# Attention and gated layers on one core: products of p and v of two pairs of units in one run, products of the first layer in pieces of one k-tile

## The chip, the cores and the metric

The kernel runs on one core of a Trainium2 chip. The metric is device time in microseconds (us), the median of several runs. Before the change it is 772.67 us (three runs: 772.47 to 773.61).

## The reference

A clustered attention over 2 x 8 heads (768 positions, 64 per head) is followed by two feed-forward blocks; all in float32.

```python
mask = q_assign[:, :, :, None] == k_assign[:, :, None, :]
scores = where(mask, (1/8) * q @ k.T, -1e9)
attn = exp(scores - max(scores)); attn = attn / (sum(attn) + 1e-9)
x = (attn @ v)                      # 16 heads -> [1536, 512]
a = x @ w1; b = x @ w2
x = (a * b @ w3) @ w_out            # d_ff 1024
h = x @ w_in                        # d_ff 2048
out = (maximum(h, 0) + alpha * minimum(h, 0)) @ w_out2
```

The assignments are the nearest of 16 centroids per head, by normalised products.

## The kernel before

**Units.** Attention is cut into 96 units: 16 heads by 6 query tiles of 128. One loop (line 762), written out by hand, gives every engine its order; an engine does its instructions in that order and waits on semaphores. In the turn of unit i TensorE (PE) transposes the weights p of unit i-4 (`emit_T`, L551, six transposes into two PSUM tiles `t` of three), then makes the scores of unit i+1 (`emit_S`, L511 and L512, four matmuls of 384 columns into a tile `s`), then possibly a step of other work ("fill"), and in even turns the products of p and v of one pair of units (`emit_PV`, L568: 12 matmuls of the program, 24 in the trace; two column tiles of 64, so the two units of a pair stand side by side in the array). The other engines: VectorE (DVE) takes the maximum of the scores (L519) and copies one half of the transposes (L559); ScalarE (ACT) does the exponential (L526) and copies the other half (L558); GpSimd (POOL) scales p by its sum (L537) and splits the next head's q and k. `emit_x` copies the products of a pair from PSUM to the rows `xr` (L580 on ACT, L581 on DVE).

**Fill.** Until unit 55 the fill steps are the cluster assignments. From unit 56 on they are the first layer of batch 0 (`l1`, L618): for every f of 8 blocks and every half a of 384 tokens one product with w1 (`l1a`) and one with w2 (`l1b`), each 4 k-tiles of three matmuls (L298 to L300, float32 split in a high and a low part), 12 matmuls in a step. The product l1a is copied from PSUM by ACT (`asb`, L627), the product l1b is multiplied with that copy by DVE (`pr`, L631). Before unit 96 both write the same tile: `alloc_f` (L679) gives the one PSUM bank `f`. All eight banks are given out: four to `s`, two to `t`, one to `o`, one to `f`. The condition in L783 puts one step in every odd unit until 16 are done (units 57 to 87); from unit 96 on there is a step in each unit, and those take turns with the two buffers of `s`.

**Weights.** `w_goal` moves the load and split of the weights on by one stage: ACT L185, L196 and L280, DVE L198, POOL L281.

After unit 103 the loop ends; the rest of the first layer and the later layers follow, TensorE work almost without a gap.

Of the kernel before, what the change touches and what calls it, by code (L numbers as in the profile page):

```python
# [8 lines left out]
F32 = mybir.dt.float32  # L9
# [7 lines left out]
B, H, S, D, NCL = 2, 8, 768, 64, 16  # L17
P = 128
NT = S // P
# [5 lines left out]
HS = S // 2  # L25
# [3 lines left out]
def kernel(  # L29
# [14 lines left out]
    nc = tc.nc  # L44

    cp = ctx.enter_context(tc.tile_pool(name="cp", bufs=1))
# [99 lines left out]
    def w_done(key):  # L146

        need[key] -= 1
# [136 lines left out]
    def w_goal(n):  # L285

        w_pairs(n)
        w_step(n)

    def w_ready(key):  # L290
        n = at[key]
        while in_ring[st["ring"]] <= n if seq[n][0] == "k" else st["conv"] <= ordinal[n]:
            w_pairs(n, True)
            if in_ring[st["ring"]] <= n or seq[n][0] == "c":
                w_step(n, True)

    def mm3(o, whi, wlo, xhi, xlo, first, last):
        nc.tensor.matmul(o, lhsT=whi, rhs=xhi, start=first, stop=False)  # L298
        nc.tensor.matmul(o, lhsT=whi, rhs=xlo, start=False, stop=False)  # L299
        nc.tensor.matmul(o, lhsT=wlo, rhs=xhi, start=False, stop=last)  # L300
# [4 lines left out]
    def pst(tag, shape, name, bufs=1):  # L305
        return ps.tile(shape, F32, tag=tag, name=name, bufs=bufs)
# [134 lines left out]
    ST, VS, hraw = {}, {}, {}  # L441

    def st_tile(name):
        return cp.tile([P, 4, S], F32R, tag="st", bufs=2, name=name)
# [8 lines left out]
    def v_load(p):  # L453
        if p < B * 4:
            VS[p] = ap.tile([P, 2, NT, D], F32, tag="vs", bufs=2, name=f"vs{p}")
            nc.sync.dma_start(out=VS[p], in_=vv[p // 4, p % 4])
# [39 lines left out]
    NU = B * H * NT  # L496
    scp, pt, sums, pth, ob, XR = {}, {}, {}, {}, {}, {}

    def unit(i):
        return i // NT, i % NT  # L500
# [21 lines left out]
    def emit_exp(i):  # L522
        if i % 2 == 0:
            sums[i // 2] = ap.tile([P, 2], F32, tag="sums", bufs=3, name=f"su{i}")
        p = ap.tile([P, S], F32, tag="p", bufs=6, name=f"p{i}")
        nc.scalar.activation(  # L526
            out=p.rearrange("p (a k) -> p a k", a=2), in_=scp.pop(i)[:, :, 0:HS], func=AF.Exp,
            bias=nmax.pop(i), scale=1.0, accum_out=sums[i // 2][:, i % 2 : i % 2 + 1],
        )
        pt[i] = p  # L530

    def emit_r(g):
        nc.vector.tensor_scalar(out=sums[g], in0=sums[g], scalar1=1e-9, scalar2=None, op0=ALU.add)
        nc.vector.reciprocal(out=sums[g], in_=sums[g])  # L534
# [8 lines left out]
    def emit_T(i):  # L543
        g, j = divmod(i, 2)
        if j == 0:
            pth[g] = ap.tile([P, NT, 256], F32, tag="pth", bufs=3, name=f"pt{g}")
        for a in range(2):
            t = pst("t", [P, 3, P], f"t{i}{a}", bufs=2)
            for k in range(3):
                kt = 3 * a + k  # L550
                nc.tensor.transpose(t[:, k], pt[i][:, kt * P : kt * P + P], ident)  # L551
            tps[i, a] = t
        pt.pop(i)
# [4 lines left out]
        nc.scalar.copy(out=pth[g][:, 0:3, q], in_=tps.pop((i, 0)))  # L558
        nc.vector.tensor_copy(pth[g][:, 3:6, q], tps.pop((i, 1)))  # L559

    def emit_PV(g):

        u, qt = unit(2 * g)
        ob[g] = pst("o", [P, P], f"o{g}")
        v = VS[u // 2]
        for kt in range(NT):
            for j in range(2):
                nc.tensor.matmul(  # L568
                    ob[g][64 * j : 64 * j + 64], lhsT=v[:, u % 2, kt], rhs=pth[g][:, kt, j * P : j * P + P],
                    start=(kt == 0), stop=(kt == NT - 1), tile_position=(0, 64 * j),  # L570
                )

    def emit_x(g):
        u, qt = unit(2 * g)
        o = ob.pop(g)
        p = u // 2
        if u % 2 == 0 and qt == 0:
            XR[p] = cp.tile([P, S], F32, tag=f"xr{p % 4}", name=f"xr{p}")
        mine = slice(0, 64) if u % 2 == 0 else slice(64, 128)
        nc.scalar.copy(out=XR[p][mine, qt * P : qt * P + P], in_=o[0:64])  # L580
        nc.vector.tensor_copy(XR[p][mine, qt * P + P : qt * P + 256], o[64:128])  # L581
        pth.pop(g)


    def lc(f, alloc, between):
# [23 lines left out]
    def l1_mm(t, b, f, m, a):  # L609
        hi, lo = his["l1", b, f, m]  # L610
        s = slice(a * HS, a * HS + HS)
        for kt in range(4):
            c = slice(kt * P, kt * P + P)
            mm3(t, hi[:, c], lo[:, c], XS[b][:, 0, kt, s], XS[b][:, 1, kt, s], kt == 0, kt == 3)
        if a == 1:
            w_done(("l1", b, f, m))

    def l1(b, f, a, alloc):  # L618

        if b == 1:  # L620
            PR[1] = PR[0]
        if b not in PR:
            PR[b] = cp.tile([P, 8 * S], F32, tag="pr", name=f"pr{b}").rearrange("p (f s) -> p f s", f=8)
        t = alloc(f"l1a{b}{f}{a}")
        l1_mm(t[:, 0:HS], b, f, 0, a)
        q = wp.tile([P, HS], F32, tag="asb", name=f"asb{b}{f}{a}")
        nc.scalar.copy(out=q, in_=t[:, 0:HS])  # L627
        yield
        t = alloc(f"l1b{b}{f}{a}")
        l1_mm(t[:, 0:HS], b, f, 1, a)  # L630
        nc.vector.tensor_tensor(out=PR[b][:, f, a * HS : a * HS + HS], in0=t[:, 0:HS], in1=q, op=ALU.mult)  # L631
        yield


    with tc.manual_schedule():
# [22 lines left out]
        for j in range(2):  # L658
            nc.vector.tensor_scalar(
                out=cpd[:, j], in0=ct, scalar1=cn2, scalar2=evod[:, j : j + 1], op0=ALU.mult, op1=ALU.mult  # L660
            )
        t = pst("s", [P, 2, 512], "cnt", bufs=2)[:, 0]
# [16 lines left out]
        def alloc_f(name):  # L679
            return pst("s", [P, 2, 512], name, bufs=2)[:, 0] if late else pst("f", [P, 512], name)  # L680

        def l1_steps(b, f, ahead):
            for a in range(2):
                if a == 0:
                    w_ready(("l1", b, f, 1))
                for _ in l1(b, f, a, alloc_f):
                    w_goal(ahead)
                    yield f

# [63 lines left out]
        nc.scalar.activation(out=warm, in_=warm, func=AF.Exp)  # L753
        nc.gpsimd.tensor_scalar(out=alp, in0=alp, scalar1=-1.0, scalar2=1.0, op0=ALU.mult, op1=ALU.mult)

        xdone, fill_at = [], [0]
        fill = fill_steps()

        LT = 4
        L1_B, L1_D = 16, 24  # L760
        NUH = NU // 2
        for i in range(NU + 8):
            if 0 <= i - LT < NU:
                emit_T(i - LT)
            if i + 1 < NU:
                emit_S(i + 1)

            if i >= 7 and i % 2 == 1 and (i - 7) // 2 < NU // 2:
                emit_x((i - 7) // 2)
            if i >= 2 and i % 2 == 0 and i // 2 - 1 < NU // 2:  # L770
                emit_r(i // 2 - 1)
            if 0 <= i - 2 < NU:
                emit_norm(i - 2)
            if 0 <= i - LT < NU:
                emit_evac(i - LT)
            if i + 1 < NU:
                emit_max(i + 1)
            if i < NU:
                emit_exp(i)
                u, j = unit(i)  # L780
                for k in ((0,), (1, 2), (3, 4), (), (5,), ())[j]:
                    h_split(u + 1, k)
            if i >= NU or i % 2 == 1 or i < 24 or 40 < i < 56:  # L783
                if fill_at[0] < (L1_B if i < NU else L1_D):
                    if next(fill) is not None:
                        fill_at[0] += 1
            fine[0] = i < NU - 1
            if 10 <= i < 54 and i % 2 == 0:
                w_goal(at["l1", 0, 2, 0])
            if NUH + 8 <= i < NU - 1 and i % 2 == 0:  # L790
                w_goal(at["l1", 0, fill_at[0] // 4, 0] + 3)
            if NUH + 4 <= i < NUH + 8:
                x_split(0, i - NUH - 4, 0)
                x_split(0, i - NUH - 4, 1)
                xdone.append(i)
            if i == NU - 1:
                late.append(i)
                for k in range(2):
                    w = st_tile(f"wo{k}").rearrange("p a n -> p (a n)").rearrange("p (g t n) -> p g t n", g=3, t=2)
                    for g in range(3):  # L800
                        WO[3 * k + g] = w[:, g, 0], w[:, g, 1]
            if i >= NU - 1:
                w_goal(at["wo", 0, 3, 0])

            k = i - 6
            if k >= 0 and k % 2 == 0 and k // 2 < NU // 2:
                emit_PV(k // 2)
                if k % 12 == 10:
                    v_load(k // 12 + 2)
        pscope.close()  # L810


# [26 lines left out]
        alloc_f = alloc_c  # L839
# [30 lines left out]
        x = cp.tile([P, 8 * S], F32, tag="wox", name="x2_1").bitcast(F32R).rearrange("p (t e s) -> p t e s", t=2, e=4)  # L870
        XF = [cp.tile([P, S], F32, tag=f"xr{e}", name=f"xf{e}") for e in range(4)]
        for b, a in ((0, 0), (0, 1), (1, 0), (1, 1)):
            s = slice(a * HS, a * HS + HS)
            for e in range(4):
                t = alloc_c(f"l2_{b}{e}{a}")
# [6 lines left out]
                if b == 1:  # L882
# [6 lines left out]
                    out=X2[b][1][:, e, s], in0=t[:, 0:HS], in1=f32(X2[b][0][:, e, s]), op=ALU.subtract  # L889
# [11 lines left out]
        x = x.rearrange("p t e s -> p (t e s)")  # L901
# [297 lines left out]
```

## Time and profile before

| | us |
|---|---|
| median of the runs | 772.67 |
| the profiled execution | 773.44 |
| its span, first to last instruction | 771.6 |
| TensorE busy in the span | 746.4 (97%) |
| VectorE, ScalarE, GpSimd busy | 464.6, 458.0, 270.1 |
| mean granted clock of TensorE | 0.99 of 2.4 GHz |

TensorE is the engine in which the time lies. Busy shares are means over the whole span; for the change the stretch of units 56 to 103 counts, about 166.8 to 309 us of the span. Matmuls are pipelined and the ends in the trace are modelled, so a matmul's cost is read from the distance of two starts. A row's start is counted from the start of the span.

### The profile page before, as it was taken

What the parts mean: (1) busy time and instruction counts of PE and PEld (TensorE: products, weight loads), DVE (VectorE), ACT (ScalarE), POOL (GpSimd) and SP (SyncE); (2) the same over time, 40 slices, a digit from 0 to 9 for tenths busy, and PEclk for the clock granted to TensorE, in tenths of its full rate; (3) what the DMA queues carried; (4) which work ended last, traced back from release to release, by engine and by line L of the source; (5) the groups of instructions that cost most, each with busy time, mean ns of one, the idle gap of its engine ahead of it and who ended that gap; (6) DMA issues with size and microseconds to landing.
All of it is one profiled execution on the core that took longest, in us unless ns stands there. A gap on an engine that the chain in (4) does not pass through costs nothing.

```text
span 771.6 us, 13292 instructions
## 1 busy us (share of the span) xinstructions
PE 746.4 (97%) x5025; PEld 675.7 (88%) x5025; DVE 464.6 (60%) x807; ACT 458.0 (59%) x946; POOL 270.1 (35%) x244
## 2 busy tenths in 40 slices
PE   5899999989999999999999999999999999999998
PEld 2787788879999989999999999999989998989886
DVE  3776798995666674357233446525645547776764
ACT  5687887675556675467344657647565544555443
POOL 0366576684555643243222432312211111221110
PEclk9799999999999999999999999999999999999999
DMA  7657466253534635756444497756655226433402
GB/s 251 193 177 224 108 173 166 67 123 79 150 110 135 186 119 168 236 217 223 160 164 164 161 316 251 282 181 231 206 201 164 110 110 232 177 114 135 163 0 82
DMA packets 39440, 129.41 MB, mean 168 GB/s; under 512 B 5232, under 2 KB 5360, under 8 KB 39376
## 3 DMA queue, kind: packets, MB, share of 16 engines
q1 hardware_dynamic: 39376, 128.56, 51.5%
q8 instruction: 40, 0.66, 0.3%
q14 instruction: 24, 0.20, 0.1%
HBM read 86.17 MB, written 28.31 MB: 148 GB/s over the span
## 4 chain that ended last, share of the span: by engine, by line
PE 86%; DMA 5%; DVE 3%; POOL 2%; ACT 2%; issue 1%; SPq 1%; POOLq 0%; ACTq 0%; DVEq 0%
PE o L568 6%; PE t L551 6%; PE l L298 6%; PE l L299 6%; PE acc L300 6%; PE acc L299 6%; PE l L300 6%; PE acc L298 6%; PE s L511 3%; PE s L512 3%; PE l1a L299 3%; PE l1b L298 3%; PE l1a L298 3%; PE l1a L300 3%; PE l1b L300 3%; PE l1b L299 3%
## 5 line engine op out<-in xcount | busy, mean ns | idle before, releaser
L281 POOL TENSOR_TENSOR wh<-wt,wh 128x512 fp32r<-128x512 f32 x57 | 74.2, 1301 | 169.7 <-ACT wh L280 165.0
L537 POOL TENSOR_SCALAR p<-p,su 128x768 f32<-128x768 f32 x96 | 88.4, 929 | 91.8 <-DVE su L534 42.4
L198 DVE SCALAR_TENSOR_TENSOR wt<-wu,wt 128x512 uint32<-128x512 uint32 x72 | 72.9, 1013 | 40.9 <-ACT wt L196 40.7
L519 DVE TENSOR_REDUCE nm<-s 128x1 f32<-128x768 f32 x96 | 91.5, 953 | 8.6 <-PE s L512 3.1
L526 ACT ACTIVATE p<-s,nm 128x768 f32<-128x768 f32 x96 | 87.1, 907 | 6.8 <-DVE nm L519 5.4
L551 PE MATMUL t<-cst,p 128*128 128x128 f32 x576 | 84.1, 281 | 3.6 <-DVE pt L559 1.6
L551 PEld LDWEIGHTS t<-cst,p 128*128 128x128 f32 x576 | 65.9, 143 | 15.8 <-issue 7.9
L511 PE MATMUL s<-st 128*128 128x384 f32 x192 | 74.9, 390 | 2.0 <-ACT p L526 1.5
L568 PE MATMUL o<-pt,vs 128*64 128x128 f32 x1152 | 73.5, 277 | 0.0
L568 PEld LDWEIGHTS o<-pt,vs 128*64 128x64 f32 x1152 | 61.9, 137 | 12.3 <-issue 12.1
L512 PE MATMUL s<-st 80*128 80x384 f32 x192 | 66.7, 347 | 0.2 <-DMA st<-mk 0.2
L558 ACT COPY pt<-t 128x384 f32<-128x384 f32 x96 | 45.9, 478 | 30.4 <-PE t L551 29.4
L559 DVE COPY pt<-t 128x384 f32<-128x384 f32 x96 | 52.8, 550 | 16.1 <-PE t L551 15.1
L244 POOL TENSOR_TENSOR sp<-sx,sp 128x512 fp32r<-128x512 f32 x16 | 22.4, 1420 | 107.9 <-ACT sp L241 107.5
L968 DVE SCALAR_TENSOR_TENSOR gr<-gr,alp 128x384 f32<-128x384 f32 x32 | 20.9, 652 | 49.1 <-ACT gr L967 49.1
L196 ACT ACTIVATE wt<-wr 128x512 uint32<-128x512 uint32 x72 | 48.3, 671 | 0.0
L185 ACT ACTIVATE wu<-wr 128x512 f32<-128x512 f32 x72 | 47.9, 666 | 0.0
L298 PE MATMUL l1a<-xs,wh 128*128 128x384 f32 x128 | 43.3, 338 | 1.3 <-DVE pr L631 0.7
L280 ACT CAST wh<-wt 128x512 fp32r<-128x512 f32 x57 | 35.4, 621 | 13.1 <-DVE wt L198 7.1
L298 PE MATMUL l1b<-xs,wh 128*128 128x384 f32 x128 | 43.1, 337 | 0.0
L299 PE MATMUL l1a<-xs,wh 128*128 128x384 f32 x128 | 43.0, 336 | 0.1
L631 DVE TENSOR_TENSOR pr<-l1b,asb 128x384 f32<-128x384 f32 x32 | 17.8, 555 | 42.1 <-PE l1b L300 24.3
(244 smaller groups left out, 1984.9 us busy)
## 6 DMA issues: line engine op xcount, KB each, us to landing
wr<-in_w_dram SPq DMA_DIRECT2D x48, 512.0 KB, 5.3
kept<-wh SPq DMA_DIRECT2D x41, 512.0 KB, 5.8
wh<-kept SPq DMA_DIRECT2D x39, 512.0 KB, 4.0
wr<-in_w3t_dram SPq DMA_DIRECT2D x16, 512.0 KB, 4.1
ywc<-kept SPq DMA_DIRECT2D x15, 512.0 KB, 3.5
jm<-in_qka_dram SPq DMA_DIRECT2D x12, 512.0 KB, 5.6
hr<-in_qkh_dram SPq DMA_DIRECT2D x16, 384.0 KB, 3.6
st<-st SPq DMA_DIRECT2D x16, 384.0 KB, 3.7
```

What stands on the lines that cost most here:

```text
L198: nc.vector.scalar_tensor_tensor(out=t, in0=u, scalar=3, in1=t, op0=ALU.logical_shift_left, op1=ALU.bitwise_or)
L281: nc.gpsimd.tensor_tensor(out=lo, in0=tts.pop(n), in1=f32(hi), op=ALU.subtract)
L298: nc.tensor.matmul(o, lhsT=whi, rhs=xhi, start=first, stop=False)
L299: nc.tensor.matmul(o, lhsT=whi, rhs=xlo, start=False, stop=False)
L300: nc.tensor.matmul(o, lhsT=wlo, rhs=xhi, start=False, stop=last)
L511: nc.tensor.matmul(t[:, a, 0:HS], lhsT=s[:, 0, q], rhs=s[:, 1, ks], start=True, stop=False)
L512: nc.tensor.matmul(t[:, a, 0:HS], lhsT=s[0:80, 2, q], rhs=s[0:80, 3, ks], start=False, stop=True)
L519: nc.vector.tensor_reduce(out=m, in_=scp[i][:, :, 0:HS], op=ALU.max, axis=AX.XY, negate=True)
L526: nc.scalar.activation(out=p.rearrange("p (a k) -> p a k", a=2), in_=scp.pop(i)[:, :, 0:HS], func=AF.Exp, bias=nmax.pop(i), scale=1.0, acc ...
L537: nc.gpsimd.tensor_scalar(out=pt[i], in0=pt[i], scalar1=sums[i // 2][:, i % 2 : i % 2 + 1], scalar2=1.0, op0=ALU.mult, op1=ALU.mult)
L551: nc.tensor.transpose(t[:, k], pt[i][:, kt * P : kt * P + P], ident)
L568: nc.tensor.matmul(ob[g][64 * j : 64 * j + 64], lhsT=v[:, u % 2, kt], rhs=pth[g][:, kt, j * P : j * P + P], start=(kt == 0), stop=(kt == N ...
```

## The change

Three edits. (1) From pair 26 on two pairs make one run: their 24 matmuls stand one behind the other at the end of a turn divisible by 4 (60, 64, ..., 100), into one tile `o` of two columns of blocks, and `emit_x` copies both together where they belong to the same head (one copy an engine, else two). In the turn behind such a run the exponential stands ahead of these copies on ACT. (2) The first layer's products give the loop back the turn after every k-tile, so a piece is three matmuls. (3) From unit 56 on pieces are given out by a counter: none in the turns divisible by 4, in the other three 6.4 / 3 each by addition (two, at times three); 64 pieces from unit 57 to unit 95, then four in every turn as before.

```diff
+    Q0 = 26
+    runs = [[g] for g in range(Q0)] + [[g, g + 1] for g in range(Q0, NU // 2, 2)]
+    run_at = {2 * r[-1] + 6: r for r in runs}
-    def emit_PV(g):
-        ob[g] = pst("o", [P, P], f"o{g}")
+    def emit_PV(r):
+        o = ob[r[-1]] = pst("o", [P, 2, P], f"o{r[0]}")
+        for k, g in enumerate(r):
...
+                        o[64 * j : 64 * j + 64, k], lhsT=v[:, u % 2, kt], rhs=pth[g][:, kt, j * P : j * P + P],
...
+            if g % 6 == 5:
+                v_load(g // 6 + 2)
...
+        for x, k in parts:
+            nc.scalar.copy(out=x[:, :, 0], in_=o[0:64, k])
+        for x, k in parts:
+            nc.vector.tensor_copy(x[:, :, 1], o[64:128, k])
...
         for kt in range(4):
+            if kt:
+                yield
             c = slice(kt * P, kt * P + P)
             mm3(t, hi[:, c], lo[:, c], XS[b][:, 0, kt, s], XS[b][:, 1, kt, s], kt == 0, kt == 3)
...
-            if i >= 7 and i % 2 == 1 and (i - 7) // 2 < NU // 2:
-                emit_x((i - 7) // 2)
+            if i - 1 in run_at:
+                if len(run_at[i - 1]) > 1 and i < NU:
+                    emit_exp(i)
+                emit_x(run_at[i - 1])
...
-            if i >= NU or i % 2 == 1 or i < 24 or 40 < i < 56:
-                if fill_at[0] < (L1_B if i < NU else L1_D):
-                    if next(fill) is not None:
-                        fill_at[0] += 1
+            if len(xdone) < 4:
+                if i % 2 == 1 or i < 24 or 40 < i < 56:
+                    next(fill)
+            else:
+                npc[0] += 0 if i % 4 == 0 and i < NU else 4 if i >= NU else 6.4 / 3
+                while npc[0] > 0.999 and fill_at[0] < (L1_B if i < NU else L1_D):
+                    npc[0] -= 1
+                    if next(fill) != "piece":
+                        fill_at[0] += 1
...
-            k = i - 6
-            if k >= 0 and k % 2 == 0 and k // 2 < NU // 2:
-                emit_PV(k // 2)
-                if k % 12 == 10:
-                    v_load(k // 12 + 2)
+            if i in run_at:
+                emit_PV(run_at[i])
```

**Place 1.** TensorE around pairs 26 and 27 (turns 58 to 61), before: `o26` and `o27` are the products of p and v, `t` transposes, `s` scores; left out stand the rest of the scores and a step of `l1b000`.

```order
L512 MATMUL s59_2302<-st9_1967 128x384
L568 MATMUL o26_2319<-pt26_2216,vs4_1701 64x128 x12
L551 MATMUL t550_2332<-cst_69,p55_2208 128x128 x3
...
L512 MATMUL s61_2377<-st10_2166 128x384
L568 MATMUL o27_2396<-pt27_2293,vs4_1701 64x128 x12
L551 MATMUL t570_2409<-cst_69,p57_2276 128x128 x3
```

The same place in the changed kernel:

```order
L512 MATMUL s61_2355<-st10_2166 128x384
L573 MATMUL o26_2374<-pt26_2216,vs4_1701 64x128 x12
L573 MATMUL o26_2374<-pt27_2285,vs4_1701 64x128 x12
L551 MATMUL t570_2399<-cst_69,p57_2276 128x128 x3
L551 MATMUL t571_2403<-cst_69,p57_2276 128x128 x3
```

The products of pair 26 moved two turns down, to those of pair 27; the scores of unit 59 are now followed by a piece and then by transposes.

**Place 2.** TensorE where the product l1a of block 1 (first half of the tokens, `l1a010`) ends and l1b (`l1b010`) begins, before, with the semaphores waited for:

```order
L300 MATMUL l1a010_2592<-xs0_2096,wh2_1194 128x384
L551 MATMUL t620_2611<-cst_69,p62_2470 128x128 [waits Activation_49,Pool_49]
...
L512 MATMUL s67_2619<-st11_2392 128x384
L568 MATMUL o30_2641<-pt30_2524,vs5_2114 64x128 x12
...
L512 MATMUL s68_2662<-st11_2392 128x384
L298 MATMUL l1b010_2679<-xs0_2096,wh3_1407 128x384
```

The same place in the changed kernel (turn 69):

```order
L300 MATMUL l1a010_2611<-xs0_2096,wh2_1194 128x384
L298 MATMUL l1b010_2734<-xs0_2096,wh3_1407 128x384 [waits Activation_49]
L299 MATMUL l1b010_2734<-xs0_2096,wh3_1407 128x384
L300 MATMUL l1b010_2734<-xs0_2096,wh3_1407 128x384
L551 MATMUL t660_2739<-cst_69,p66_2598 128x128 [waits PE_49,Pool_49]
```

Two turns of transposes, scores and products stood between the last matmul of l1a and the first of l1b; now none does, and the first of l1b has a wait for ACT.

**Place 3.** DVE where the product l1b of block 1, first half, is multiplied (`pr`, with the copy `asb010`), before; `nm68` is the maximum of the scores `s68`:

```order
L559 COPY pt31_2610<-t631_2658 128x3x128
L519 TENSOR_REDUCE nm68_2673<-s68_2662 128x1
L631 TENSOR_TENSOR pr0_490<-l1b010_2679,asb010_2605 128x384
L533 TENSOR_SCALAR su66_2631<-su66_2631 128x2
L534 RECIPROCAL su66_2631<-su66_2631 128x2
```

The same place in the changed kernel (turn 71):

```order
L559 COPY pt33_2738<-t671_2774 128x3x128
L519 TENSOR_REDUCE nm72_2786<-s72_2778 128x1
L651 TENSOR_TENSOR pr0_490<-l1b010_2734,asb010_2729 128x384
L533 TENSOR_SCALAR su70_2759<-su70_2759 128x2
L534 RECIPROCAL su70_2759<-su70_2759 128x2
```

The multiplication (L631, now L651) moved four units down and stands, as before, directly behind the maximum of its turn.

## Rows read from the trace of the kernel before

**Rows 1.** Stretches: PE, PEld, DVE, ACT, POOL busy, clock, DMA share, GB/s.
```profile
184.46:268.18 83.72, 83.72 (x730) 77.77 (x729) 54.19 (x102) 50.03 (x113) 46.82 (x46) 1.00 0.52 142
268.18:289.19 21.01, 20.62 (x196) 18.35 (x195) 15.82 (x32) 15.46 (x35) 9.88 (x11) 1.00 0.39 118
```

**Rows 2.** All waits of PE from 180 to 310 us: total, times, longest.
```profile
PE t L551 <- ACT pt L558: 0.3, 1, 0.3
```

**Rows 3.** Order of time, PE, a pair with a step of l1: start, us, instruction.
```profile
202.05 0.34 PE L512 MATMUL s<-st 80*128 80x384 f32 x1
202.32 1.53 PE L568 MATMUL o<-pt,vs 128*64 128x128 f32 x24
...
204.41 0.42 PE L511 MATMUL s<-st 128*128 128x384 f32 x1
...
210.85 0.42 PE L511 MATMUL s<-st 128*128 128x384 f32 x1
```

**Rows 4.** Order of time, PE, a unit without products of p and v.
```profile
275.86 0.34 PE L512 MATMUL s<-st 80*128 80x384 f32 x1
276.05 0.82 PE L551 MATMUL t<-cst,p 128*128 128x128 f32 x6
276.63 0.44 PE L511 MATMUL s<-st 128*128 128x384 f32 x1
```

**Rows 5.** The last 22 matmuls of the run of 24 at 202.32.
```profile
202.48 1.37 PE L568 MATMUL o<-pt,vs 128*64 128x128 f32 x22
```

**Rows 6.** Order of time, PE and ACT, the end of a step of l1a.
```profile
200.69 0.34 PE L300 MATMUL l1a<-xs,wh 128*128 128x384 f32 x1
200.87 0.38 PE L551 MATMUL t<-cst,p 128*128 128x128 f32 x2
...
201.07 0.48 ACT L627 COPY asb<-l1a 128x384 f32<-128x384 f32 x1 [1.77 <-PE l1a L300]
```

**Rows 7.** Order of time, PE and DVE, two steps without anything between, behind the loop.
```profile
313.27 0.34 PE L300 MATMUL l1b<-xs,wh 128*128 128x384 f32 x1
...
313.64 0.56 DVE L631 TENSOR_TENSOR pr<-l1b,asb 128x384 f32<-128x384 f32 x1 [0.25 <-PE l1b L300]
...
314.35 0.41 PE L298 MATMUL l1a<-xs,wh 128*128 128x384 f32 x1 [0.74 <-DVE pr L631]
...
314.60 0.34 PE L299 MATMUL l1a<-xs,wh 128*128 128x384 f32 x1
```

**Rows 8.** Order of time, PE and DVE, scores, a step of l1b, the maximum.
```profile
205.02 0.34 PE L512 MATMUL s<-st 80*128 80x384 f32 x1
205.20 0.34 PE L298 MATMUL l1b<-xs,wh 128*128 128x384 f32 x1
...
205.40 0.96 DVE L519 TENSOR_REDUCE nm<-s 128x1 f32<-128x768 f32 x1
```

**Rows 9.** Order of time, PE, the two late transposes of units without fill.
```profile
280.41 1.10 PE L551 MATMUL t<-cst,p 128*128 128x128 f32 x6
...
289.19 0.41 PE L551 MATMUL t<-cst,p 128*128 128x128 f32 x2 [0.33 <-ACT pt L558]
```

**Rows 10.** Costliest groups: busy us, mean ns of one, idle before.
```profile
L526 ACT ACTIVATE p<-s,nm 128x768 f32<-128x768 f32 x96 | 87.1, 907 | 6.8 <-DVE nm L519 5.4
...
L568 PE MATMUL o<-pt,vs 128*64 128x128 f32 x1152 | 73.5, 277 | 0.0
...
L185 ACT ACTIVATE wu<-wr 128x512 f32<-128x512 f32 x72 | 47.9, 666 | 0.0
...
L280 ACT CAST wh<-wt 128x512 fp32r<-128x512 f32 x57 | 35.4, 621 | 13.1 <-DVE wt L198 7.1
```

**Rows 11.** Stretches of 5 us, for the granted clock (columns as in rows 1).
```profile
25.00:30.00 5.00, 3.51 (x13) 3.12 (x14) 4.10 (x7) 3.25 (x7) 1.74 (x1) 0.64 0.69 200
30.00:35.00 5.00, 4.84 (x18) 4.15 (x17) 4.71 (x11) 3.13 (x7) 1.95 (x3) 0.50 0.56 138
313.00:318.00 5.00, 4.26 (x25) 3.97 (x24) 1.12 (x3) 2.09 (x5) 1.28 (x1) 1.00 0.83 277
```

More of the change, by code (lines that the diff above doesn't have):

```diff
@@ L559, in emit_evac @@
         nc.vector.tensor_copy(pth[g][:, 3:6, q], tps.pop((i, 1)))
-    def emit_PV(g):
-        u, qt = unit(2 * g)
-        ob[g] = pst("o", [P, P], f"o{g}")
[L565 to L582, printed above, removed]
+    Q0 = 26
@@ new lines @@
+    runs = [[g] for g in range(Q0)] + [[g, g + 1] for g in range(Q0, NU // 2, 2)]
[3 more added lines that the diff above has]
+        for k, g in enumerate(r):
+            u, qt = unit(2 * g)
+            v = VS[u // 2]
+            for kt in range(NT):
+                for j in range(2):
+                    nc.tensor.matmul(
+                        o[64 * j : 64 * j + 64, k], lhsT=v[:, u % 2, kt], rhs=pth[g][:, kt, j * P : j * P + P],
+                        start=(kt == 0), stop=(kt == NT - 1), tile_position=(0, 64 * j),
+                    )
+            if g % 6 == 5:
+                v_load(g // 6 + 2)
@@ new lines, in emit_x @@
+    def emit_x(r):
+        o = ob.pop(r[-1])
+        parts = []
+        for k, g in enumerate(r):
+            u, qt = unit(2 * g)
+            p = u // 2
+            if u % 2 == 0 and qt == 0:
+                XR[p] = cp.tile([P, S], F32, tag=f"xr{p % 4}", name=f"xr{p}")
+            x = XR[p][0:64] if u % 2 == 0 else XR[p][64:128]
+            x = x.rearrange("p (t q) -> p t q", q=P)
+            pth.pop(g)
+            if parts and parts[0][2] == u:
+                parts[0] = x0[:, qt - 2 : qt + 2], slice(0, 2), u
+            else:
+                parts.append((x[:, qt : qt + 2], slice(k, k + 1), u))
+            x0 = x
+        parts = [(x.rearrange("p (k j) q -> p k j q", j=2), k) for x, k, _ in parts]
+        for x, k in parts:
+            nc.scalar.copy(out=x[:, :, 0], in_=o[0:64, k])
+        for x, k in parts:
+            nc.vector.tensor_copy(x[:, :, 1], o[64:128, k])
@@ L624, in l1 @@
         t = alloc(f"l1a{b}{f}{a}")
-        l1_mm(t[:, 0:HS], b, f, 0, a)
+        yield from l1_mm(t[:, 0:HS], b, f, 0, a)
         q = wp.tile([P, HS], F32, tag="asb", name=f"asb{b}{f}{a}")
         nc.scalar.copy(out=q, in_=t[:, 0:HS])
-        yield
+        yield 0
         t = alloc(f"l1b{b}{f}{a}")
-        l1_mm(t[:, 0:HS], b, f, 1, a)
+        yield from l1_mm(t[:, 0:HS], b, f, 1, a)
         nc.vector.tensor_tensor(out=PR[b][:, f, a * HS : a * HS + HS], in0=t[:, 0:HS], in1=q, op=ALU.mult)
-        yield
+        yield 0
     with tc.manual_schedule():
@@ L680, in alloc_f @@
             return pst("s", [P, 2, 512], name, bufs=2)[:, 0] if late else pst("f", [P, 512], name)
+        pieces = [True]
         def l1_steps(b, f, ahead):
@@ L685, in l1_steps @@
                     w_ready(("l1", b, f, 1))
-                for _ in l1(b, f, a, alloc_f):
+                for done in l1(b, f, a, alloc_f):
+                    if done is None:
+                        if pieces[0]:
+                            yield "piece"
+                        continue
                     w_goal(ahead)
@@ L754 @@
         nc.gpsimd.tensor_scalar(out=alp, in0=alp, scalar1=-1.0, scalar2=1.0, op0=ALU.mult, op1=ALU.mult)
-        xdone, fill_at = [], [0]
+        xdone, fill_at, npc = [], [0], [0]
         fill = fill_steps()
@@ L778 @@
             if i < NU:
-                emit_exp(i)
+                if len(run_at.get(i - 1, ())) < 2:
+                    emit_exp(i)
                 u, j = unit(i)
@@ L782 @@
                     h_split(u + 1, k)
-            if i >= NU or i % 2 == 1 or i < 24 or 40 < i < 56:
-                if fill_at[0] < (L1_B if i < NU else L1_D):
-                    if next(fill) is not None:
+            if len(xdone) < 4:
+                if i % 2 == 1 or i < 24 or 40 < i < 56:
+                    next(fill)
+            else:
+                npc[0] += 0 if i % 4 == 0 and i < NU else 4 if i >= NU else 6.4 / 3
+                while npc[0] > 0.999 and fill_at[0] < (L1_B if i < NU else L1_D):
+                    npc[0] -= 1
+                    if next(fill) != "piece":
                         fill_at[0] += 1
@@ L803 @@
                 w_goal(at["wo", 0, 3, 0])
-            k = i - 6
-            if k >= 0 and k % 2 == 0 and k // 2 < NU // 2:
-                emit_PV(k // 2)
-                if k % 12 == 10:
-                    v_load(k // 12 + 2)
+            if i in run_at:
+                emit_PV(run_at[i])
+        pieces[0] = False
         pscope.close()
```

## The prediction

> **What bounds the kernel now.** I read first the busy shares by stretch. From 184.46 to 268.18 us, where one step of the first layer falls on each pair of units, TensorE is busy for 83.72 of 83.72 us, while DVE, ACT and POOL have 54, 50 and 47 us; in the units behind it, without fill, it is 20.62 of 21.01 us [rows 1]. Ends of matmuls are modelled, so this could hide short waits. The list of waits therefore comes next: from 180 to 310 us, units 61 to 103, TensorE has one entry, 0.3 us [rows 2]. And in order of time the starts repeat: scores of a pair begin at 204.41 and of the next at 210.85 us, 6.44 us a pair [rows 3]. So in this stretch the time is the sum of TensorE's own distances from start to start. An instruction taken from it, or a wait put into it, counts in full; what the other engines save counts nothing. Nobody waits for the copy `asb` or the product `pr`: neither stands in rows 2.
>
> **The change, part by part.**
>
> *Two pairs in one run.* From the last matmul of the scores to the first of the next scores, with a pair of products between, is 204.41 - 202.05 = 2.36 us [rows 3]; without it 276.63 - 275.86 = 0.77 us [rows 4]. Inside the run, the last 22 matmuls cover 1.37 us, of which one matmul's own length is 0.28 us [rows 5, 10]: 1.09 us for ten distances between couples, 0.109 each, 1.31 us for twelve. The remaining 2.36 - 0.77 - 1.31 = 0.28 us are the price of going into the column tiles and out of them. A run of 24 and a run of 48 pay it once each: 22 pairs become 11 runs, 11 x 0.28 = 3.1 us less.
>
> The Trainium skill, page "TensorEngine Tiling (Array Packing)", section "Key Properties", says that a change of the tiling mode drains the engine while a change of the tile alone does not. By that, too, the seam between the two pairs inside a run is free, and the 0.28 us above are the trace's price of the drain, for which the page has no figure here.
>
> *The copies behind a run.* `emit_x` saves 7 copies on each of ACT and DVE. These are not on TensorE's path: nothing. The exponential now stands ahead of them in the turn behind a run; its scores are older than the run and a run lasts some 2.9 us, against 0.91 us for the exponential [rows 10], so the run hides it. Without that cover the copy of the transposes behind it would be late by up to 0.91 us, eleven times at worst; this I put into the rival with late engines.
>
> *Pieces instead of steps.* Cutting costs no join: scores to l1 0.18 us (205.02 to 205.20) [rows 8], l1 to transposes 0.18 us (200.69 to 200.87) [rows 6], scores to transposes 0.19 us [rows 4], and the matmuls and weights are the same. What it buys is that the units 88 to 95, formerly without fill, get some. There the trace shows two late transposes: 1.10 instead of 0.82 us for six, 0.28 us [rows 9, 4], and 0.33 us for an ACT copy [rows 9]. Both go at best: 0.6 us less. There is no other idle time to fill.
>
> *The new waits.* This is the part on which the forecast rests. Pieces are counted, not aligned: turns hold two, at times three, so that after the first three-piece turn (pieces 15 to 17) a turn can hold the last piece of one product and the first of the next. Both products use the one bank `f`, so the second waits until ACT has copied, or DVE multiplied, the first, and every transpose and score behind it on TensorE waits as well. Place 2 shows one such place: last matmul of l1a, then at once the first of l1b with a wait for ACT. In the kernel before the same two are two turns apart. By the counter the ends of pieces 16, 20, 24, 28 and 48, 52, 56, 60 fall inside a turn: eight places, of which 20, 28, 52, 60 are ends of l1a (ACT) and 16, 24, 48, 56 ends of l1b (DVE). The other ends fall on the end of a turn, where transposes and scores of 1.4 us (0.77 + 0.61 [rows 3, 4, 8]) stand between.
>
> The price from rows. For DVE one such place lies behind the loop: last matmul at 313.27, multiplication at 313.64 for 0.56 us, next matmul at 314.35 [rows 7]. That is 1.08 us instead of the usual 0.17, and the next distance is 0.25 instead of 0.17: 0.98 us lost. For ACT the copy begins 0.38 us behind the last matmul and takes 0.48 us [rows 6]; with the 0.15 us from DVE's end to TensorE's start in rows 7 that makes 1.01 instead of 0.17 us, with the slow first matmul 0.91 us lost. For DVE the maximum of the turn comes first (place 3): it starts 0.38 us behind the last matmul of the scores and lasts 0.96 us [rows 8]. Where two pieces stand between scores and boundary (16, 48) it is over in time: 0.98 us each. Where only one does (24, 56), the last matmul of the piece starts 0.52 us behind the scores; the multiplication starts at about 1.34, ends at 1.90, TensorE goes on at 2.05 instead of 0.70: 1.35 plus 0.08, 1.43 us each. Sum: 4 x 0.91 + 2 x 0.98 + 2 x 1.43 = 8.5 us. The bounds: eight times the least gap that rows 6 and 7 allow, 0.84 us, is 6.7; eight times the greatest, 1.43, is 11.4. I take 8.5, since each place has its own row. A cost below 6.7 would need a second place for the product, and there is no bank left.
>
> *Sum.* 8.5 - 3.1 - 0.6 = +4.8 us: 773.44 becomes 778.2 for an execution like the profiled one. That one lies 0.77 us above the median of the three, so for the median 772.67 + 4.8 = 777.5 us.
>
> **Rivals.**
>
> *The waits cost nothing and the gains stay (faster).* 772.67 - 3.1 - 0.6 = 769.0 us. For it: `asb` and `pr` were never waited for, and ACT and DVE are idle for a third of the stretch [rows 1]. Against it: at the eight places nothing stands on TensorE between the last matmul and the one that overwrites its bank. It decides if the tile of the second product does not have to wait for the first one's reader.
>
> *Only some of the waits show.* If half of the eight were found covered, the sum is 4.2 - 3.7 = +0.5, 773.2 us, no change that could be told. Against it: none of the eight has a cover.
>
> *The other engines come late too (slower still).* A turn without a run is now 0.77 us for the transposes with their joins [rows 4], 0.61 us from the first to the last matmul of the scores (204.41 to 205.02) [rows 3, 8] and 1.05 us for two pieces of three matmuls at 0.175: 2.4 us, against a mean of 3.2 before (6.44 for two). ACT's exponential, 0.91, with two copies of 0.48 and two weight stages of 0.67 and 0.62 us [rows 6, 10] is 3.2 us, 0.8 over. About five blocks of weights fall in this stretch; 5 x 0.8 adds 4 at most, and I put 2: 779.5 us. The mean speaks against it: the four turns of a group (1.4 us of transposes and scores in each, 6.4 pieces at 0.53, a run at 2.9) still last 11.9 us.
>
> *The clock.* Before, the clock was at its lower level, 0.50, in 30 to 35 us, after a stretch in which TensorE was busy for 3.51 of 5 us; in 313 to 318, with 4.26 of 5 and the wait of rows 7 in it, it stayed 1.00 [rows 11]. The eight waits are of that last size. If the clock fell all the same, each group of four turns in it would take some 11.9 us more, about 789 us for one.
> The Trainium skill, page "TensorE: Matmul & The Clock Gate", section "A second HAM failure mode: psum-queue depth-cycling", tells of a kernel whose short pauses between groups of matmuls, over PSUM banks, made the clock go up and down. By that rule the eight waits would do it; the row from 313 us speaks against it.
>
> **Chances.** Forecast 0.71, with a range of its own from 775.7 (least waits) to 780.2; other engines late 0.13; waits that cost nothing 0.08; some of the waits 0.06; clock 0.02. About 0.2%, 1.55 us, is what a measurement of this kernel can tell from no change: slower 0.86, within 0.06, faster 0.08. For 8 in 10 the range goes from 774.6 to 780.6; the faster case stays outside.
>
> **What would show it.** In the profile after: TensorE's waits list four entries of l1a for `pr` and four of l1b for `asb` in the stretch, each about 0.7 to 1.2 us idle; eleven runs of 48 matmuls with 2.36 + 1.31 us around them; no late transposes in units 92 and 95; granted clock 1.00 there. The stretch behind unit 103 keeps its length. I am wrong if those waits are missing or below 0.4 us, if the runs do not save 0.28 us each, or if TensorE waits for p, t or s instead.

## The result and the profile after

The changed kernel takes 776.65 us (median of 13 runs) against 772.67 us before (13 runs): ratio 1.0054, 95% interval 1.0043 to 1.0064, slower by some 4 us. Forecast were 777.5 us and slower.

The profiled execution took 775.21 us with a span of 773.4 us, 1.8 us more than before. The spans hide 2 us: up to the first transpose in the turn of unit 57 the program is the same, yet from the first matmul on it took 167.2 us before and 165.4 us in this execution. So the comparison is made from that transpose to the last product of p and v. Stretches (as rows 1: PE, PEld, DVE, ACT, POOL busy, clock, DMA), first units 57 to 95, then 96 to the last product; before:

```profile
171.58:289.19 117.61, 117.22 (x1034) 108.09 (x1035) 78.27 (x150) 71.63 (x162) 62.87 (x62) 1.00 0.47 128
289.19:306.90 17.71, 17.71 (x156) 16.54 (x156) 7.11 (x15) 9.73 (x21) 6.08 (x5) 1.00 0.51 176
```

and after:

```profile
169.53:289.93 120.40, 114.84 (x1010) 107.37 (x1011) 74.03 (x141) 70.15 (x153) 61.23 (x61) 1.00 0.43 116
289.93:308.60 18.67, 18.67 (x179) 17.92 (x179) 8.47 (x16) 11.09 (x23) 7.38 (x6) 1.00 0.71 226
```

135.3 us became 139.1, 3.8 us more. TensorE does less work in it (133.5 instead of 134.9 us busy), but is no longer busy throughout: 5.6 of the 120.4 us are idle. From the last product of p and v to the last matmul there are 460.7 us in both traces. The clock stays at 1.00. What TensorE waited for in this stretch of the changed kernel (total, times, longest), the answer to [rows 2]:

```profile
PE l1a L298 <- DVE pr L651: 3.3, 4, 1.0
PE l1b L298 <- ACT asb L647: 2.3, 4, 0.6
PE t L551 <- POOL p L537: 1.1, 1, 1.1
```

The third entry is the wait ahead of the first transpose of turn 57, which the list of before has too, with the same 1.1 us. The first two are new: four and four.

A run of two pairs in order of time, beside [rows 3]:

```profile
202.61 0.33 PE L512 MATMUL s<-st 80*128 80x384 f32 x1
202.87 2.84 PE L573 MATMUL o<-pt,vs 128*64 128x128 f32 x48
205.64 0.87 PE L551 MATMUL t<-cst,p 128*128 128x128 f32 x6
206.27 0.42 PE L511 MATMUL s<-st 128*128 128x384 f32 x1
```

From scores to scores 3.66 us, of which 0.77 are the transposes and 24 couples at 0.109 us make 2.62: 0.27 us for going in and out, once for two pairs.

The end of l1a inside turn 69 (place 2), TensorE and ACT:

```profile
207.06 0.34 PE L298 MATMUL l1a<-xs,wh 128*128 128x384 f32 x1
...
207.41 0.34 PE L300 MATMUL l1a<-xs,wh 128*128 128x384 f32 x1
207.78 0.48 ACT L647 COPY asb<-l1a 128x384 f32<-128x384 f32 x1 [1.08 <-PE l1a L300]
...
208.31 0.45 PE L298 MATMUL l1b<-xs,wh 128*128 128x384 f32 x1 [0.57 <-ACT asb L647]
...
208.60 0.34 PE L299 MATMUL l1b<-xs,wh 128*128 128x384 f32 x1
```

0.90 us from one matmul to the next instead of 0.175, then 0.29 instead of 0.175: 0.84 us lost. The list of waits shows 0.57 for it, since modelled ends count a part as busy; the starts show the whole.

The end of l1b inside turn 71 (place 3), TensorE and DVE:

```profile
212.56 0.34 PE L512 MATMUL s<-st 80*128 80x384 f32 x1
...
212.93 0.96 DVE L519 TENSOR_REDUCE nm<-s 128x1 f32<-128x768 f32 x1
...
213.08 0.34 PE L300 MATMUL l1b<-xs,wh 128*128 128x384 f32 x1
213.80 0.55 DVE L651 TENSOR_TENSOR pr<-l1b,asb 128x384 f32<-128x384 f32 x1
...
214.41 0.44 PE L298 MATMUL l1a<-xs,wh 128*128 128x384 f32 x1 [0.99 <-DVE pr L651]
214.69 0.34 PE L299 MATMUL l1a<-xs,wh 128*128 128x384 f32 x1
```

The maximum keeps DVE until the multiplication can begin at 213.80; TensorE loses 1.15 us here and 0.1 us at the next matmul, 1.25 us.

The last piece of a product is called its end here; an end stands inside a turn when the first piece of the next product follows it in the same turn. By the starts of the transposes, a turn with two pieces and no such end lasts 2.48 us right behind a run and 2.41 to 2.44 elsewhere, one with three 2.94 us. Turns 66 and 86 last 3.86 (DVE, two pieces ahead), 69, 74, 89 and 94 last 3.31, 3.25, 3.31 and 3.26 (ACT; 69 and 89 stand behind a run), 71 and 91 last 3.67 us (DVE, one piece ahead). Against their like, the eight excesses add up to 2 x 0.92 + 4 x 0.83 + 2 x 1.23 (1.25 by the matmuls of turn 71 above) = 7.6 us.

### The profile page after: what moved, and what is told of

Same layout as the page of the kernel before. It is cut to its first block, busy times and chain, and to the rows that moved or that the text cites. A ratio compares the mean times of both kernels' runs of the same rounds, so it can differ in the third digit from the quotient of the medians.

```text
span 773.4 us, 13278 instructions
## 1 busy us (share of the span) xinstructions
PE 743.9 (96%) x5025; PEld 675.4 (87%) x5025; DVE 461.6 (60%) x800; ACT 456.8 (59%) x939; POOL 269.6 (35%) x244
## 4 chain that ended last, share of the span: by engine, by line
PE 88%; DVE 3%; ACT 3%; DMA 2%; POOL 1%; issue 1%; SPq 1%; POOLq 0%; ACTq 0%; DVEq 0%
PE o L573 7%; PE t L551 7%; PE l L300 6%; PE l L298 6%; PE acc L300 6%; PE acc L299 6%; PE l L299 6%; PE acc L298 6%; PE s L511 4%; PE s L512 3%; PE l1a L298 3%; PE l1b L298 3%; PE l1a L299 3%; PE l1a L300 3%; PE l1b L300 3%; PE l1b L299 3%
## 5 line engine op out<-in xcount | busy, mean ns | idle before, releaser
L551 PE MATMUL t<-cst,p 128*128 128x128 f32 x576 | 82.5, 278 | 3.5 <-DVE pt L559 1.9
L573 PE MATMUL o<-pt,vs 128*64 128x128 f32 x1152 | 71.1, 276 | 0.0
L298 PE MATMUL l1a<-xs,wh 128*128 128x384 f32 x128 | 43.8, 342 | 4.6 <-DVE pr L651 4.0
L185 ACT ACTIVATE wu<-wr 128x512 f32<-128x512 f32 x72 | 47.8, 664 | 0.0
L299 PE MATMUL l1a<-xs,wh 128*128 128x384 f32 x128 | 43.0, 336 | 0.1
L280 ACT CAST wh<-wt 128x512 fp32r<-128x512 f32 x57 | 35.4, 621 | 13.1 <-DVE wt L198 7.1
L300 PE MATMUL l1a<-xs,wh 128*128 128x384 f32 x128 | 43.0, 336 | 0.0
```

Source lines behind the costliest of these rows:

```text
L573: nc.tensor.matmul(o[64 * j : 64 * j + 64, k], lhsT=v[:, u % 2, kt], rhs=pth[g][:, kt, j * P : j * P + P], start=(kt == 0), stop=(kt == NT ...
```

## The experiments

All start from the changed kernel. The times of the stretch go from the first transpose of turn 57 to the last product of p and v, by the starts in each trace. The ratio compares means with executions of the kernel before that were taken beside each kernel.

| kernel | median us | ratio to before (95%) | stretch us | to before |
|---|---|---|---|---|
| before | 772.67 | 1 | 135.3 | |
| changed | 776.65 | 1.0054 (1.0043 to 1.0064) | 139.1 | +3.8 |
| e1, aligned pieces | 768.28 | 0.9945 (0.9926 to 0.9964) | 131.4 | -3.9 |
| e2, runs alone | 774.42 | 1.0016 (1.0005 to 1.0028) | 137.4 | +2.1 |
| e3, pieces alone | 779.26 | 1.0078 (1.0063 to 1.0093) | 142.2 | +6.9 |
| e4, all ends inside | 785.62 | 1.0167 (1.0150 to 1.0184) | 146.5 | +11.2 |
| e6, aligned, no runs | 771.78 | 0.9989 (0.9977 to 1.0001) | 134.6 | -0.7 |

**e1, aligned pieces.**

```diff
-                npc[0] += 0 if i % 4 == 0 and i < NU else 4 if i >= NU else 6.4 / 3
+                npc[0] += 0 if i % 4 == 0 and i < NU else 4 if i >= NU or i in (57, 77) else 2
```

> The changed kernel with one line altered: pieces are given out as 2 in each of three turns of four (4 in turns 57 and 77), so that every product of the first layer ends at the end of a turn and 0 of 16 ends stand inside one; runs, pieces and everything else stay. Theory A (the loss is the wait for the one bank f at ends inside a turn, 7.6 us by the trace of the changed kernel): no wait of l1a for pr or of l1b for asb before unit 96, and 776.65 - 7.6 = 769.0 us, 0.5% faster than before. Rival B (cutting the products into pieces, or the shorter turns with other engines behind, cost the time): the cuts and the short turns are still there, so 776 to 777 us. Rival C (the copies and the exponential in other order around the runs of two cost it): 776 to 777 us.

Measured 768.28 us, 0.55% faster than before. All that the list of TensorE's waits in the stretch holds is the entry ahead of turn 57, and the stretch of units 57 to 95 is busy throughout:

```profile
PE t L551 <- POOL p L537: 1.1, 1, 1.1
```

```profile
170.13:282.84 112.71, 112.71 (x1010) 107.82 (x1011) 74.84 (x141) 68.91 (x152) 61.53 (x61) 1.00 0.46 124
```

The stretch falls by 7.7 us against the changed kernel; the eight waits were 7.6. Theory A stands; B and C fall, for cuts, short turns, copies and the place of the exponential are the same here.

**e4, all ends inside a turn.**

```diff
-                npc[0] += 0 if i % 4 == 0 and i < NU else 4 if i >= NU else 6.4 / 3
+                npc[0] += 0 if i % 4 == 0 and i < NU else 4 if i >= NU or i in (77, 87) else 1 if i == 57 else 3 if i == 95 else 2
```

> The changed kernel with one line altered: 1 piece in turn 57, 2 in the others (4 in turns 77 and 87, 3 in turn 95), so that 15 of 16 ends of products stand inside a turn, each with one piece ahead of it in the turn: 8 ends of l1a and 7 of l1b. Theory A: the trace of the changed kernel has 0.83 us lost at such an end of l1a and 1.25 us at one of l1b: 8 x 0.83 + 7 x 1.25 = 15.4 us instead of 7.6, so 776.65 + 7.8 = 784.4 us. Rivals B and C: as many pieces, runs and turns as in the changed kernel, so 776 to 777 us.

Measured 785.62 us, and 7.4 us more in the stretch than the changed kernel where 7.8 were expected. The waits in the stretch:

```profile
PE l1a L298 <- DVE pr L651: 6.7, 7, 1.1
PE l1b L298 <- ACT asb L647: 4.5, 8, 0.6
PE t L551 <- POOL p L537: 1.1, 1, 1.1
```

Seven and eight, as counted. Of the seven ends of l1b one, in turn 77, has three pieces ahead of it and not one; that turn is 0.92 us longer than its like in e1, as turns 66 and 86 of the changed kernel, and not the 1.25 us of the expectation. The loss follows the number of ends inside turns, with the same number of pieces.

**e2, runs alone.**

```diff
-        pieces = [True]
+        pieces = [False]
...
-                npc[0] += 0 if i % 4 == 0 and i < NU else 4 if i >= NU else 6.4 / 3
-                while npc[0] > 0.999 and fill_at[0] < (L1_B if i < NU else L1_D):
-                    npc[0] -= 1
-                    if next(fill) != "piece":
-                        fill_at[0] += 1
+                if (i >= NU or i % 2 == 1) and fill_at[0] < (L1_B if i < NU else L1_D):
+                    next(fill)
+                    fill_at[0] += 1
```

> The changed kernel with the runs of two pairs, but whole steps of the first layer in every odd turn as before the change. Theory A: 11 runs save 11 x 0.28 = 3.1 us and nothing waits for bank f; the turns 88 to 95 stay without fill: 772.67 - 3.1 = 769.6 us, 769 to 771. Rival B (pieces cost): the same 769.6. Rival C (the runs of two cost, by copies, exponential or buffers): 773 us or more.

A miss, by theory A and by B: 774.42 us instead of 769.6, which is where rival C had put it. The trace shows how the runs cost here: a turn between two steps that holds neither a step nor a run lasts 1.37 us, and there the other engines come late. TensorE, ACT and DVE around turn 66, where this is the case:

```profile
202.04 0.82 PE L551 MATMUL t<-cst,p 128*128 128x128 f32 x6
...
202.24 0.48 ACT L647 COPY asb<-l1a 128x384 f32<-128x384 f32 x1 [2.66 <-PE l1a L300]
...
202.62 0.42 PE L511 MATMUL s<-st 128*128 128x384 f32 x1
202.62 0.68 ACT L185 ACTIVATE wu<-wr 128x512 f32<-128x512 f32 x1
...
202.90 0.56 DVE L559 COPY pt<-t 128x384 f32<-128x384 f32 x1 [0.93 <-PE t L551]
...
203.20 0.47 ACT L558 COPY pt<-t 128x384 f32<-128x384 f32 x1
...
203.56 0.91 ACT L526 ACTIVATE p<-s,nm 128x768 f32<-128x768 f32 x1
...
203.60 0.85 PE L551 MATMUL t<-cst,p 128*128 128x128 f32 x6
...
204.61 0.45 PE L511 MATMUL s<-st 128*128 128x384 f32 x1 [0.17 <-ACT p L526]
```

ACT does the copy `asb` and a weight stage (L185) first, so its copy of the transposes runs only from 203.20 to 203.67. The next transposes start at 203.60 instead of 203.41 (202.04 + 1.37), before that copy ends: what released them is DVE's copy, done at 203.45, since in this turn the first of them go into the tile that DVE empties. ACT's exponential, from 203.56, holds up the next scores until 204.61. Turns 66 and 67 are 0.19 and 0.36 us longer than 58 and 59, whose TensorE work is the same, and about as much longer are 74 and 75, 78 and 79, 82 and 83, 86 and 87. In all five ACT has a weight stage between `asb` and its copy; in turns 62 and 70 it has none, and they last 1.37 us as turn 58. Turns 91 and 92 are 0.6 and 0.9 us longer than their like, 95 is 0.7 longer than before the change. That makes 4.9 of the 5.2 us which the stretch loses (137.4 against 135.3 - 3.1). That the even spreading is what lets the runs pay is read from this against e1; how much each of the late engines weighs was not tried apart.

**e3, pieces alone.**

```diff
-    Q0 = 26
+    Q0 = NU // 2
```

> The changed kernel with the pieces and their counter, but each pair of products in a run of its own in every even turn as before. Theory A: the eight waits stay (7.6 us), the late transposes of units 92 and 95 go (0.6), nothing is saved at the runs: 772.67 + 7.0 = 779.7 us. Rival B gives the same sign, without waits for f as its cause. Rival C (the runs cost): 772 to 773 us.

779.26 us: as expected by theory A, with four and four waits of the same 3.3 and 2.3 us in the list. Without the runs the stretch is 3.1 us longer than in the changed kernel (142.2 against 139.1), so the runs of two are not the cause of the loss there.

**e6, aligned pieces without runs** (the edits of e1 and e3 together).

> The kernel with aligned pieces, each pair in a run of its own. Theory A: no waits for f, no gain at the runs, only the late transposes of units 92 and 95 gone: 772.67 - 0.6 = 772.1 us; equally 768.28 + 3.1 = 771.4. Between 771 and 772.5. Were the gain of the aligned kernel due to even spreading alone and not to the drains, it would be 768 to 769 us here too.

771.78 us, 0.7 us less than before in the stretch: the late transposes of the units without fill, and no more. The step from here to e1 is 134.6 - 131.4 = 3.2 us for eleven runs fewer, 0.29 us each.

**e7, the maximum behind the pieces in turns 71 and 91.**

```diff
-            if i + 1 < NU:
+            if i + 1 < NU and i not in (71, 91):
                 emit_max(i + 1)
...
+            if i in (71, 91):
+                emit_max(i + 1)
```

> The changed kernel, in turns 71 and 91 with the maximum of the next scores behind the pieces instead of ahead, so that DVE multiplies l1b (ends of pieces 24 and 56) first. One look at the trace: by theory A the distance of turn 71 to 72 and of 91 to 92 falls from 3.67 to about 3.3 us (the loss from 1.25 to 0.9), that of the other six stays (3.86, 3.31, 3.25 us). If the maximum were not what is ahead of the multiplication, they stay at 3.67.

One execution, 775.93 us. Turn 71, TensorE, then DVE:

```profile
214.36 0.34 PE L300 MATMUL l1b<-xs,wh 128*128 128x384 f32 x1
215.41 0.44 PE L298 MATMUL l1a<-xs,wh 128*128 128x384 f32 x1 [0.72 <-DVE pr L651]
```

```profile
214.80 0.56 DVE L651 TENSOR_TENSOR pr<-l1b,asb 128x384 f32<-128x384 f32 x1 [0.74 <-PE l1b L300]
215.28 0.95 DVE L519 TENSOR_REDUCE nm<-s 128x1 f32<-128x768 f32 x1
```

Both turns last 3.40 us instead of 3.67, the other six are unchanged within 0.05. The maximum ahead of the multiplication is what made the two ends dearer.

**e8 and e5, aligned pieces and runs from pair 14 or pair 2 on** (`Q0 = 14`, `Q0 = 2` in e1).

> The kernel with aligned pieces, with runs of two from pair 14 on: 6 runs fewer. 768.28 - 6 x 0.28 = 766.6 us if TensorE sets the pace from unit 34 on; no gain or up to 2 us more if the turns without pieces are too short for ACT and DVE there. I expect 768.

> The kernel with aligned pieces, with runs of two pairs from pair 2 on instead of 26: 12 runs fewer. If TensorE set the pace there too, 12 x 0.28 = 3.4 us less: 768.28 - 3.4 = 764.9 us. But between units 12 and 56 the turns between two runs have no pieces: 1.4 us of TensorE against 1.6 us of ACT (0.91 + 0.20 + 0.48), as in the kernel with runs alone, where 5.2 us were lost so in units 57 to 95; by that 767 to 771 us. I expect the second: 768.5.

772.82 us (ratio to before 1.0002, 0.9989 to 1.0014) and 776.32 us (1.0039, 1.0023 to 1.0055): both lose what e1 had won, more than I expected, e8 by 5 us and e5 by 8. From turn 57 on both are as e1 (112.71 us for units 57 to 95 in each). From the first matmul to turn 57 they take 170.3 and 172.3 us against 165.9 in e1, but 165.4 to 169.0 occur in the traces whose program is the same up to there, and in e8 2.8 of the 4.5 us over e1 lie ahead of turn 8, where no run has been moved yet. So the transposes of turns 32 and 57 are compared: between them lie 63.6 to 63.9 us in the eight traces with single pairs there, 66.5 in e8 and 68.2 in e5. The medians lie further from e1's, 4.5 and 8.0 us; where the rest comes from stays open. TensorE's waits of the transposes for the two copies, from 50 to 176 us in e5:

```profile
PE t L551 <- DVE pt L559: 3.7, 7, 1.0
PE t L551 <- ACT pt L558: 1.7, 2, 1.0
```

and from 50 to 170 us in e1:

```profile
PE t L551 <- DVE pt L559: 1.9, 3, 0.8
```

In turn 44 of e5 the granted clock also falls to 0.50, its lower level (1.2 of 2.4 GHz). TensorE in that turn, and then the stretch ahead of the fall and the one at the lower level, with columns as in [rows 1]:

```profile
139.32 0.55 PE L551 MATMUL t<-cst,p 128*128 128x128 f32 x3 [0.66 <-ACT pt L558]
...
141.83 0.69 PE L406 MATMUL jd<-cst,pr 128*128 128x128 f32 x3 [1.24 <-DVE pr L396]
142.45 4.32 PE L573 MATMUL o<-pt,vs 128*64 128x128 f32 x48
```

```profile
138.16:142.10 3.94, 2.03 (x13) 1.46 (x12) 3.94 (x5) 2.10 (x5) 3.77 (x4) 1.00 0.33 71
142.10:145.50 3.40, 3.40 (x33) 3.09 (x33) 2.34 (x5) 1.47 (x3) 2.63 (x3) 0.50 0.48 108
```

TensorE was busy for 2.03 of 3.94 us ahead of the fall, and the run of 48 then takes 4.32 us instead of 2.84: 1.5 of the 4.5 us that e5 loses between turns 32 and 57.

Without pieces to fill the turns between, runs of two go with more waiting for the copies there, as in e2; that this and the clock are the whole of the loss is not shown. e1 is the fastest of these kernels and beats both the one before and the changed one.

## Why the prediction was right

- **What bounds.** From unit 57 on TensorE's starts set the time: taking away 7.6 us of waits took 7.7 us from the stretch (e1), fifteen of them instead of eight added 7.4 (e4).
- **The new waits**, the term that decided. The eight places were read from the order and the counter, and are the eight of the trace. The size was a little too high: 7.6 us instead of 8.5. From the reader's end to TensorE's next start 0.05 us pass (207.78 + 0.48 to 208.31), where 0.15 was taken from [rows 7]. There the first matmul waits for its weights as well, which I overlooked; ACT's cast of them (L280) is done at 314.04 (313.42 + 0.62), ahead of DVE at 314.20, so it is not the last to come, but it is no case of one wait alone. The multiplication starts 1.24 us behind the scores, not 1.34, since DVE begins it before the maximum has ended. In the list of waits an end of l1a shows 0.57 us, below the 0.7 to 1.2 that was to be seen, for the modelled ends hide a part.
- **Two pairs in one run**: 0.28 us each, 3.1 in all; measured 3.2 (e6 to e1) and 3.1 (e3 to the changed kernel).
- **Late transposes**: 0.6 forecast, 0.7 measured (e6).
- **Sum**: 7.6 - 3.2 - 0.7 = +3.7 against +3.8 in the stretch and +4.0 in the medians; forecast +4.8. The bounds of the range come from the waits, 6.7 and 11.4 us; the greater gives 780.4 us, where the prediction has 780.2.
- **Pieces.** That cutting costs no join held (turns of 2.41 to 2.48 us, e1 busy throughout). That it buys nothing but the late transposes was too little said: with runs of two, whole steps lose 5.2 us (e2). In the changed kernel this does not show, since the pieces are there; the forecast did not hang on it, but the rival with late engines had its mechanism right for e2, and wrong for the changed kernel.
- **Rivals.** Waits without a cost, or some of them covered: no, all eight show. Clock: in the stretch it is 1.00 in the changed kernel and with fifteen waits in e4 (116.56 of 127.85 us busy). The row of 25 to 30 us that the prediction sets ahead of the fall [rows 11] has itself a mean of 0.64, so the clock fell inside it, and the row does not show what TensorE did before the fall. The Trainium skill, page "TensorE: Matmul & The Clock Gate", section "A second HAM failure mode: psum-queue depth-cycling", tells of another kernel (bf16, 512 columns) in which short pauses of TensorE between groups of matmuls made the clock go up and down; the waits of this stretch did not, at 1.00 throughout. Ahead of turn 57, in e5, it did fall once, behind the waits of turn 44.

## What to carry to other kernels

Where two products take turns on one PSUM bank, what matters of a finer interleaving is where their ends fall: an end with other matmuls behind it is free, an end with the next product right behind it costs the reader's time on an engine that did not wait there before (0.83 to 1.23 us here). Count these places in the order before counting the gain; here one line, which puts them at the ends of turns, turned 4 us lost into 4 us won. And a longer run pays only while the turns between stay long enough for the other engines (e2, e5, e8).

## What was not expected of the hardware

The first matmul behind such a wait is followed 0.28 to 0.29 us later by the next, instead of 0.175 (turns 69 and 71), so a wait costs about 0.1 us more than itself; [rows 7] had 0.25 there. The wait is not needed for it: where a product starts behind transposes without a wait, the distance is 0.26 us, as in this place of the changed kernel.

```profile
290.51 0.42 PE L298 MATMUL l1a<-xs,wh 128*128 128x384 f32 x1
290.77 0.34 PE L299 MATMUL l1a<-xs,wh 128*128 128x384 f32 x1
```

And 48 column-tiled matmuls in one run keep the pace of 0.109 us a couple across the change from one pair to the next: the seam is free (2.84 us for all 48), as the prediction had it.
